# A decode block on one core: 112-column quadrants, a folded second mean, and differently cut MLP weight loads

## The chip, the core and the metric

The kernel runs on one core of a Trainium2 chip. The metric is the device time in microseconds (us) of one execution, the median over the timed runs. Engines are named as the profile names them: PE is TensorE's matmul side and PEld its weight loads, DVE is VectorE, ACT is ScalarE, POOL is GpSimd, SP is SyncE, which here only issues DMAs. "SPq" is SP's queue of issued work.

## The reference

Four sequences (B = 4) with one new token each go through an attention over the last 1024 cached positions and then through an MLP. Both have a layer norm ahead of them and a residual sum behind them; the MLP is normalised twice, once outside and once inside.

```python
B, Sq, D = 4, 1, 448; Hq, Hkv, Sk, Dh = 16, 8, 4096, 256; F = 1792
W = min(4096, max(256, Sk // 4))                      # 1024
q = layernorm(x) @ wq
k, v = k_cache[:, :, Sk - W:], v_cache[:, :, Sk - W:] # 8 kv heads, each for two q heads
o = softmax(q @ k.T * Dh ** -0.5) @ v
h = x + o @ wo
y = layernorm(layernorm(h))
out = h + gelu(y @ w1 + b1) @ w2 + b2
```

All tensors are float32. K and V of the window are 33.6 MB each; with the weights some 88 MB are read once.

## The kernel before, in words

**Loading.** All large inputs come over SP's queue, in the order in which they are used. Twelve packed pieces called "stream" (`LOADS`, issued in `part`, L97) hold wq, K, V and wo of the heads in the order of their use; behind them come the last V (`v7`, two transfers), the last two heads' wo (`wo67`), the first MLP weights `w1` in two transfers (L373) and the second ones `w2` in four (L376). They go into a ring of three slots of equal size; a transfer into a slot is issued when the slot's last reader is done, so three slots' worth of transfers are under way or waiting at any time. Nothing else orders the loads.

**Heads.** For each of the 8 kv heads PE multiplies q by K (`scores`, L224), transposes the probabilities (L249), multiplies them by V (`values`, L261), transposes the result (`heads`, L286) and multiplies by wo (`project_o`). The order of PE's instructions is the order in which the program writes them; the other engines' order is set by the scheduler. A group of small products on zeros (`keep_warm`, L341) keeps PE busy between pieces of real work near the end.

**The tail.** The block's vector h has 4 x 448 numbers. They lie on 128 partitions: four quadrants of 32 partitions, one for each quarter j of the columns, with one of every 8 partitions holding a real row. In the kernel before a quadrant holds 128 columns: the quarters are columns 0 to 127, 128 to 255, 256 to 383, and 384 to 447 twice (64 columns, doubled by the function `columns`). Row sums over all quadrants come from a product with `fold`, which counts the doubled quarter by one half.

After the last wo product (`hsum`), DVE adds x and takes row sums (`h`, L411), PE turns these into the mean (L402), DVE subtracts it (`d`, L416), PE makes the second mean from the sums of d (L402), DVE subtracts it too (`z`, L421), PE transposes z by a product with picked columns of the identity (`pz`, L426), and DVE copies it into `zT` (L427), the weights of the first MLP product. ACT squares d and z for the two variances, which become the scale s beside the first MLP product (L438), and s is applied to the product's result together with b1 (L451), ahead of the GELU on ACT (L452).

The first MLP product runs over four slices of the 448 rows of w1. They are 128, 128, 128 and 64 rows; the last 64 rows are stored in two halves of columns on partitions 0 to 63 and 64 to 127 (`packed`), so that w1 fills 128 partitions x 6272 columns. The result u is transposed (`put`, L457 and L459), copied into `gT` (L461, L463) and multiplied by the 14 chunks of w2 (`py`, L469), 128 rows of w2 each, four products of 32 partitions a chunk. DVE adds h + b2 (`res`, L473) and SP stores the result (L474).

Of the kernel before, what the change touches and what calls it, by code (L numbers as in the profile page):

```python
# [8 lines left out]
F32 = mybir.dt.float32  # L9
# [6 lines left out]
B, D = 4, 448  # L16
# [14 lines left out]
QU = KV // 4  # L31
X0 = 2 * ND * B
V7A = 6 * B * DH
# [29 lines left out]
SLOT = max(sum(map(width, parts)) for parts in LOADS)  # L63
W1C = 3 * F + F // 2
EPS = 1e-5
# [3 lines left out]
def block_kernel(ctx: ExitStack, tc, rows, first, streams, v7, wo67, w1, w2, out):  # L69
# [82 lines left out]
    for j in range(4):  # L152
        nc.vector.tensor_scalar_mul(fold[: 3 * Q, j, :], sel[: 3 * Q, :], 1.0 / D)
        nc.vector.tensor_scalar_mul(fold[3 * Q :, j, :], sel[3 * Q :, :], 0.5 / D)
    fold = fold.rearrange("p j q -> p (j q)")
# [9 lines left out]

    b2b = const.tile([P, P], F32, name="b2b")
    nc.gpsimd.memset(b2b, 0.0)
    nc.scalar.dma_start(b2b[::GAP, :], rows)
    rs = const.tile([P, P + FQ], F32, name="rs")

    def spread(t):
        return t[..., ::GAP]
    xb, b1b = rs[:, :P], rs[:, P:]

# [96 lines left out]
    def columns(t, j):  # L271
        if j < 3:
            return t[:, j * P : (j + 1) * P].rearrange("p (i c) -> p i c", i=2)
        return t[:, None, 3 * P :].to_broadcast([t.shape[0], 2, H])

# [17 lines left out]
    def project_o(g, wt):  # L293
        for i in range(4):
            if g < HKV - 2:
                nc.tensor.matmul(  # L296
                    acc[i * Q : (i + 1) * Q, :], oT[g % 2][:, i, :], wt[:, i, :],
                    start=(g == 0), stop=(g == HKV - 3),
                )
                continue  # L300
            for j in range(4):
                nc.tensor.matmul(
                    ph[j * Q : (j + 1) * Q], oT[g % 2][:, i, :], columns(wt[:, i, :], j),
                    start=False, stop=(g == HKV - 1 and i == 3),
                )
# [14 lines left out]

    b1T = t0[:, WC + ND * B :].rearrange("p (c j) -> p c j", c=4)
    nc.vector.tensor_copy(spread(zT), xT)
    b1s = work.tile([P, 2 * 512], F32, tag="p", name="b1s")[:, : 4 * P]
# [8 lines left out]
    px = ps_s.tile([P, 512], F32, tag="s", name="px")  # L332
    nc.tensor.transpose(px[:, :P], zT.rearrange("p j q -> p (j q)"), ident)
    nc.vector.tensor_copy(xb, px[:, :P])

    tail = []

    def keep_warm(n, to=None):
        to = tail[0][:, 0, :] if to is None else to
        for _ in range(n):  # L340
            nc.tensor.matmul(to[:Q, :512], idle[:, :Q], idle, start=True, stop=True)  # L341
# [5 lines left out]
    for g in range(HKV):  # L347
        if g + 1 < HKV:
            p, rec_next = scores(g + 1)
            if g + 2 < HKV:  # L350
                project_q(g + 2, wq_parts(part("q", g + 2)))
            transpose_p(g + 1, p)
            if g + 1 == HKV - 2:
                keep_warm(10, ps_m.tile([P, 512], F32, tag="m", name="wait"))
            if g + 1 == HKV - 1:
                keep_warm(2, ps_m.tile([P, 512], F32, tag="m", name="wait"))
                tail.append(ps_t.tile([P, 2, 512], F32, tag="t", name="tail"))
                accs = once.tile([P, D], F32, tag="u", name="accs")
                nc.scalar.copy(accs, acc)
                keep_warm(8)  # L360
                hsum = ps_s.tile([P, 512], F32, tag="s", name="hsum")[:, :P]
                ph = hsum.rearrange("p (i c) -> p i c", i=2)
                pu = ps_s.tile([P, 512], F32, tag="s", name="pu")[:, :FQ]
                for j in range(4):
                    nc.tensor.matmul(ph[j * Q : (j + 1) * Q], sel, columns(accs, j), start=True, stop=False)
        else:
            v7t = load_v7()
            tw = slot("w1")
            wo_last = [wo_rows(tw[:, i * WC : (i + 1) * WC]) for i in range(2)]
            nc.sync.dma_start(tw[:, : 2 * WC], wo67)  # L370
            tw1 = tw[:, 2 * WC : 2 * WC + W1C]
            for a, n in ((0, 2 * F), (2 * F, W1C - 2 * F)):
                nc.sync.dma_start(tw1[:, a : a + n], w1[:, a : a + n])  # L373
            tw2 = slot("w2")
            for c0, n in ((0, 8), (8, 3), (11, 2), (13, 1)):
                nc.sync.dma_start(tw2[:, c0 * D : (c0 + n) * D], w2[:, c0 * D : (c0 + n) * D])  # L376
        if g == HKV - 1:
            keep_warm(8)
        po = values(g, v7t if g == HKV - 1 else None)
        heads(g, po, rec)  # L380
        if g < HKV - 2:
            project_o(g, wo_rows(part("o", g)))
        if g == HKV - 1:
            keep_warm(5)
            for i in range(2):
                project_o(HKV - 2 + i, wo_last[i])
        if g + 1 < HKV:
            rec = rec_next

    w1t = [tw1[:, a * F : (a + 1) * F] for a in range(3)] + [tw1[:, 3 * F :]]  # L390
    w2t = [tw2[:, c * D : (c + 1) * D] for c in range(NFC)]


    def w1_part(a, j):
        if a < 3:
            return slice(0, P), w1t[a][:, FQ * j : FQ * (j + 1)]
        rows = slice(H * (j // 2), H * (j // 2) + H)
        return rows, w1t[a][rows, FQ * (j % 2) : FQ * (j % 2 + 1)]


    def row_mean(sums, at, name):
        nc.tensor.matmul(at, fold, sums, start=True, stop=True)  # L402
        return at

    def stat(name):
        return once.tile([P, 1], F32, tag=name, name=name)

    keep_warm(3)
    h = once.tile([P, P], F32, tag="h", name="h")
    hs, ds, dv, zv = (stat(n) for n in ("hs", "ds", "dv", "zv"))  # L410
# [3 lines left out]
    keep_warm(2)  # L414
    d = once.tile([P, P], F32, tag="dh", name="dh")
    nc.vector.tensor_scalar(d, h, m, None, op0=ALU.subtract, op1=ALU.add, accum_out=ds)  # L416
    pm2 = ps_m.tile([P, 2], F32, tag="m", name="pm2")
    m = row_mean(ds, pm2[:, 0:1], "m2")
    keep_warm(2)
    z = once.tile([P, P], F32, tag="z", name="z")  # L420
    nc.vector.tensor_scalar(z, d, m, None, op0=ALU.subtract)  # L421
    junk = once.tile([P, P], F32, tag="junk", name="junk")
# [3 lines left out]
    nc.tensor.matmul(pz, z, rows_of, start=True, stop=True)  # L426
    nc.vector.tensor_copy(spread(zT), pz)  # L427
    hb = once.tile([P, P], F32, tag="hb", name="hb")
# [6 lines left out]
    for a in range(ND):  # L435
        for j in range(4):
            rows, w = w1_part(a, j)
            nc.tensor.matmul(  # L438
                pu[j * Q : (j + 1) * Q, :], zT[rows, a, :], w, start=(a == 0), stop=(a == ND - 1),
            )  # L440
        if a == 0:
            rsqrt(r1, row_mean(dv, tail[0][:, 1, 0:1], "v1"), "r1")
        if a == 1:
            v2 = stat("v2")
            nc.vector.tensor_scalar(v2, row_mean(zv, tail[0][:, 1, 1:2], "v2"), r1, r1, op0=ALU.mult, op1=ALU.mult)
            rsqrt(s, v2, "r2")
            nc.vector.tensor_mul(s, s, r1)


    for cols in (slice(0, 2 * P), slice(2 * P, FQ)):  # L450
        nc.vector.scalar_tensor_tensor(u[:, cols], pu[:, cols], s, b1b[:, cols], op0=ALU.mult, op1=ALU.add)  # L451
        nc.scalar.activation(u[:, cols], u[:, cols], AF.Gelu_apprx_tanh)  # L452

    keep_warm(5)
    put = ps_m.tile([P, 4, 4, B], F32, tag="m", name="put")
    for c in range(3):
# [5 lines left out]
    for i, rows in enumerate((slice(0, H), slice(H, P))):  # L462
        nc.vector.tensor_copy(spread(gT[rows, 12:, :]), put[rows, 3].rearrange("p (j i) q -> p j i q", i=2)[:, :, i, :])  # L463
    py = ps_o.tile([P, 2, H], F32, tag="o", name="py")
    for c in range(NFC):
        for j in range(4):
            n = 2 if c == 0 or j < 3 else 1
            w = columns(w2t[c], j) if n == 2 else w2t[c][:, None, 3 * P :]
            nc.tensor.matmul(  # L469
                py[j * Q : (j + 1) * Q, :n, :], gT[:, c, :], w, start=(c == 0), stop=(c == NFC - 1),  # L470
            )
    res = once.tile([P, P], F32, tag="res", name="res")
    nc.vector.tensor_add(res, py.rearrange("p i c -> p (i c)"), hb)  # L473
    nc.sync.dma_start(out, res)  # L474
# [73 lines left out]
```

## Time and profile before

| what | value |
|---|---|
| median of 3 runs (lowest, highest) | 214.31 us (214.24, 214.54) |
| time of the profiled execution | 214.15 us |
| its span, first to last instruction | 212.4 us |
| PE busy / DVE / ACT / POOL, share of the span | 70% / 17% / 12% / 2% |
| share of the DMA engines' time taken by SP's queue | 97.0% |
| mean transfer rate over the span | 416 GB/s |
| mean granted TensorE clock | 0.871 |

A span begins with the core's first instruction and ends with its last; the execution's time has 1.75 us more around it. A row of the timeline gives the start, the length, the engine, the line, the operation, what is written and read, the shape and the count; in brackets stands how long the engine had been idle before it and what ended that. "DMA w<-w" as the releaser means the landing of a transfer into one of the weight tiles.

### The profile page before, as it was taken

What the parts mean: (1) busy time and instruction counts of PE and PEld (TensorE: products, weight loads), DVE (VectorE), ACT (ScalarE), POOL (GpSimd) and SP (SyncE); (2) the same over time, 40 slices, a digit from 0 to 9 for tenths busy, and PEclk for the clock granted to TensorE, in tenths of its full rate; (3) what the DMA queues carried; (4) which work ended last, traced back from release to release, by engine and by line L of the source; (5) the groups of instructions that cost most, each with busy time, mean ns of one, the idle gap of its engine ahead of it and who ended that gap; (6) DMA issues with size and microseconds to landing.
All of it is one profiled execution on the core that took longest, in us unless ns stands there. A gap on an engine that the chain in (4) does not pass through costs nothing.

```text
span 212.4 us, 2546 instructions
## 1 busy us (share of the span) xinstructions
PE 148.5 (70%) x1102; PEld 57.2 (27%) x1102; DVE 36.2 (17%) x149; ACT 24.6 (12%) x58; POOL 5.1 (2%) x17
## 2 busy tenths in 40 slices
PE   0478815832891883980794780686999999999994
PEld 0332301300211520230222220141343334335443
DVE  1520310400111110320113011031130031101220
ACT  2011300300002100030003000030030102000310
POOL 5100000000000000000000000000000000000110
PEclk9999985995578599797579699599699999999999
DMA  7999899999989999999999999999999999999991
GB/s 296 438 406 509 350 499 414 427 436 418 479 385 464 427 414 430 417 479 403 446 446 403 446 414 461 426 426 397 454 412 426 432 423 415 424 416 424 424 386 67
DMA packets 3354, 88.45 MB, mean 416 GB/s; under 512 B 384, under 2 KB 656, under 8 KB 1040
## 3 DMA queue, kind: packets, MB, share of 16 engines
q1 hardware_dynamic: 3312, 88.29, 97.0%
q8 instruction: 8, 0.13, 0.2%
q14 instruction: 2, 0.02, 0.0%
q10 hardware_dynamic: 32, 0.01, 0.0%
HBM read 88.24 MB, written 0.07 MB: 416 GB/s over the span
## 4 chain that ended last, share of the span: by engine, by line
DMA 81%; PE 15%; SPq 1%; DVE 1%; issue 0%
DMA stream<-stream 70%; DMA w<-w 11%; PE s L224 6%; PE po L261 4%; PE acc L296 2%; PE pot L286 1%; PE pq L199 1%; PE py L469 0%; DVE o L278 0%; SPq L97 0%; SPq L376 0%; DVE oT L291 0%; SPq L95 0%; DVE res L473 0%
## 5 line engine op out<-in xcount | busy, mean ns | idle before, releaser
L224 PE MATMUL s<-stream,qT 128*32 128x512 f32 x256 | 40.0, 772 | 18.1 <-DMA stream<-stream 18.1
L261 PE MATMUL po<-stream,pT 128*32 128x512 f32 x224 | 30.6, 685 | 16.3 <-DMA stream<-stream 16.3
L224 PEld LDWEIGHTS s<-stream,qT 128*32 128x32 f32 x256 | 10.2, 139 | 45.1 <-issue 31.1
L228 DVE TENSOR_REDUCE mx<-s 128x1 f32<-128x512 f32 x16 | 11.1, 692 | 62.9 <-PE s L224 62.9
L261 PEld LDWEIGHTS po<-stream,pT 128*32 128x32 f32 x224 | 7.1, 120 | 33.4 <-DMA stream<-stream 18.9
L199 PE MATMUL pq<-stream,yT 128*32 128x512 f32 (+1 forms) x80 | 10.7, 630 | 7.6 <-DMA stream<-stream 4.7
L201 ACT COPY qs<-pq 128x512 f32<-128x512 f32 x8 | 4.7, 585 | 76.7 <-PE pq L199 76.7
L278 DVE TENSOR_SCALAR o<-po,rec 128x256 f32<-128x256 f32 x8 | 3.9, 484 | 54.9 <-PE po L261 54.9
L235 ACT ACTIVATE p<-s,nm 128x512 f32<-128x512 f32 x16 | 10.9, 689 | 15.8 <-DVE nm L231 15.8
L279 ACT ACTIVATE o<-po,rec 128x256 f32<-128x256 f32 x8 | 3.8, 474 | 69.6 <-DVE o L278 69.6
L249 PE MATMUL ppt<-ident,p 128*128 128x128 f32 x64 | 11.1, 303 | 0.2
L341 PEld LDWEIGHTS <-idle 128*32 128x32 bf16 x85 | 7.5, 96 | 11.5 <-issue 4.7
L286 PE MATMUL pot<-ident,o 128*128 128x128 f32 x32 | 7.7, 337 | 3.8 <-DVE o L278 3.1
L207 PE MATMUL pqt<-ident,qs 128*128 128x128 f32 x32 | 6.1, 323 | 5.6 <-ACT qs L201 5.6
L341 PE MATMUL tail<-idle 128*32 128x512 bf16 x37 | 9.4, 381 | 0.0
L296 PE MATMUL acc<-stream,oT 128*32 128x448 f32 x48 | 7.5, 698 | 2.5 <-DVE oT L291 1.4
L249 PEld LDWEIGHTS ppt<-ident,p 128*128 128x128 f32 x64 | 7.6, 151 | 3.8 <-ACT p L235 3.8
L199 PEld LDWEIGHTS pq<-stream,yT 128*32 128x32 f32 x80 | 4.4, 128 | 15.4 <-issue 14.5
L286 PEld LDWEIGHTS pot<-ident,o 128*128 128x128 f32 x32 | 3.6, 157 | 13.3 <-DVE o L278 10.7
L207 PEld LDWEIGHTS pqt<-ident,qs 128*128 128x128 f32 x32 | 3.9, 159 | 10.2 <-ACT qs L201 8.5
L193 POOL TENSOR_TENSOR r<-ve_r,mhalf 128x1 f32<-128x1 f32 x2 | 1.1, 543 | 191.5 <-DVE ve_r L192 191.5
L210 DVE TENSOR_REDUCE q<-pqt 128x16 f32<-128x64 f32 x8 | 1.8, 224 | 16.8 <-PE pqt L207 16.8
(110 smaller groups left out, 79.1 us busy)
## 6 DMA issues: line engine op xcount, KB each, us to landing
stream<-stream SPq DMA_DIRECT2D x5, 7040.0 KB, 39.1
stream<-stream SPq DMA_DIRECT2D x2, 6912.0 KB, 40.5
stream<-stream SPq DMA_DIRECT2D x2, 4992.0 KB, 24.3
stream<-stream SPq DMA_DIRECT2D x2, 4096.0 KB, 24.1
stream<-stream SPq DMA_DIRECT2D x1, 5888.0 KB, 36.4
w<-w SPq DMA_DIRECT2D x2, 1792.0 KB, 23.1
v<-v SPq DMA_DIRECT2D x1, 3072.0 KB, 20.1
w<-wo SPq DMA_DIRECT2D x1, 1792.0 KB, 20.1
```

What stands on the lines that cost most here:

```text
L199: nc.tensor.matmul(pq[j * Q : (j + 1) * Q, cols], yT[:, a, :], w, start=True, stop=True)
L201: nc.scalar.copy(qs, pq)
L207: nc.tensor.transpose(pt[:, i * P : (i + 1) * P], qs[:, i * P : (i + 1) * P], ident)
L224: nc.tensor.matmul(s[h][b * Q : (b + 1) * Q, :], qT[g % 2][:, c, b, :], load_k(g, h, c)[:, b, :], start=(c == 0), stop=(c == 1),)
L228: nc.vector.reduce_max(mx[:, h : h + 1], s[h], axis=AX.X)
L235: nc.scalar.activation(p[:, h * 512 : (h + 1) * 512], s[h], AF.Exp, bias=nm, scale=SCALE, accum_out=sums[:, h : h + 1],)
L249: nc.tensor.transpose(pt[:, c, :], p[:, c * P : (c + 1) * P], ident)
L261: nc.tensor.matmul(po[b * Q : (b + 1) * Q], pT[g % 2][:, c, b, :], vt[:, :, b, :], start=(c == 0), stop=(c == NKC // 2 - 1),)
L278: nc.vector.tensor_scalar_mul(o[:, :, :P], po[:, :, :P], rec)
L286: nc.tensor.transpose(pt[:, at : at + P], o[:, i, c * P : (c + 1) * P], ident)
L296: nc.tensor.matmul(acc[i * Q : (i + 1) * Q, :], oT[g % 2][:, i, :], wt[:, i, :], start=(g == 0), stop=(g == HKV - 3),)
L341: nc.tensor.matmul(to[:Q, :512], idle[:, :Q], idle, start=True, stop=True)
```

## The change

Four things are changed together.

1. **Quadrants of 112 columns.** 448 = 4 x 112, so each quadrant now holds a true quarter and no column is doubled. `fold` is the same in all rows. The products into `hsum` and `py` are 112 columns wide for each quadrant, and DVE's and ACT's operations of the tail work on 112 columns. x is carried a second time in the first load, cut in quarters of 112 (16 more columns of 128 rows). The result keeps its 128 columns in the store; the 16 behind are zeros that POOL writes ahead of time.
2. **The second mean is subtracted inside the transposing product.** PE transposes d rather than z, and a second product that accumulates into the same `pz` subtracts the second mean (weights from the sums of d, and `foldn`, which is the negative of `fold`). z itself is still made for its variance, behind.
3. **w1 on 112 partitions.** Four slices of 112 rows, 112 partitions x 7168 columns, in two transfers of 4608 and 2560 columns. The third slice's first 256 columns of each quarter come with the first transfer.
4. **w2 in pieces of 8, 4, 1.5 and 0.5 chunks** in place of 8, 3, 2 and 1. The last chunk's product is made in two halves of 56 columns.

```diff
-X0 = 2 * ND * B
+X0 = 3 * ND * B
+C = D // 4
-W1C = 3 * F + F // 2
+W1C = 4 * F
+W1A = 2 * F + 4 * 2 * P
...
+    foldn = const.tile([P, 4, B], F32, name="foldn")
+    nc.vector.tensor_scalar_mul(foldn, fold.rearrange("p j (b e) -> p j b e", b=B)[..., 0], -1.0)
...
-            for a, n in ((0, 2 * F), (2 * F, W1C - 2 * F)):
-                nc.sync.dma_start(tw1[:, a : a + n], w1[:, a : a + n])
+            for a, e in ((0, W1A), (W1A, W1C)):
+                nc.sync.dma_start(tw1[:C, a:e], w1[:, a:e])
...
-            for c0, n in ((0, 8), (8, 3), (11, 2), (13, 1)):
-                nc.sync.dma_start(tw2[:, c0 * D : (c0 + n) * D], w2[:, c0 * D : (c0 + n) * D])
+            for a, e in ((0, 16), (16, 24), (24, 27), (27, 28)):
+                nc.sync.dma_start(tw2[:, a * 2 * C : e * 2 * C], w2[:, a * 2 * C : e * 2 * C])
...
+    pz = ps_m.tile([P, 4, B], F32, tag="m", name="pz")
+    nc.tensor.matmul(pz[:C], d, rows_of, start=True, stop=False)
+    nc.tensor.matmul(pz[:C], ds.to_broadcast([P, C]), foldn, start=False, stop=True)
+    nc.vector.tensor_copy(spread(zT[:C]), pz[:C])
     pm2 = ps_m.tile([P, 2], F32, tag="m", name="pm2")
     m = row_mean(ds, pm2[:, 0:1], "m2")
-    keep_warm(2)
...
-    pz = ps_m.tile([P, 4, B], F32, tag="m", name="pz")
-    nc.tensor.matmul(pz, z, rows_of, start=True, stop=True)
-    nc.vector.tensor_copy(spread(zT), pz)
...
-    keep_warm(2)
+    keep_warm(4)
...
+    for a, half in ((2, 0), (2, 1), (3, None)):
+        first_layer(a, half)
...
+    for half in range(2):
+        for j in range(4):
+            nc.tensor.matmul(
+                py[j * Q : (j + 1) * Q, half * C // 2 : (half + 1) * C // 2], gT[:, NFC - 1, :],
+                w2_last[half][:, j * C // 2 : (j + 1) * C // 2], start=False, stop=(half == 1),
+            )
+    nc.vector.tensor_add(res[:, :C], py, hb)
```

SP issues the same transfers in the same order; the last of them differ in shape. From `wo67` on they stood like this before (a "w" tile is w1's or w2's slot, the shape is partitions x elements of 4 bytes):

```order
L370 DMA w_937<-wo 128x3584
L373 DMA w_937<-w 128x3584
L373 DMA w_937<-w 128x2688
L376 DMA w_941<-w 128x3584
L376 DMA w_941<-w 128x1344
L376 DMA w_941<-w 128x896
L376 DMA w_941<-w 128x448
L474 DMA out<-res 128x128
```

and now:

```order
L371 DMA w_935<-wo 128x3584
L374 DMA w_935<-w 112x4608
L374 DMA w_935<-w 112x2560
L377 DMA w_939<-w 128x3584
L377 DMA w_939<-w 128x1792
L377 DMA w_939<-w 128x672
L377 DMA w_939<-w 128x224
L489 DMA out<-res 128x128
```

The two transfers of w1 hold as many bytes as before on 16 partitions fewer, with rows of 18432 and 10240 bytes in place of 14336 and 10752; the last transfer of w2 is half as long.

On PE, from the second mean to the first MLP product (`ds` are the sums of d, `pz` the transposed vector, `tail<-idle` the small products on zeros), there stood before:

```order
L402 MATMUL pm_1036<-ds,fold 128x1
L341 LDWEIGHTS idle
L341 MATMUL tail<-idle 32x512
L341 LDWEIGHTS idle
L341 MATMUL tail<-idle 32x512
L426 MATMUL pz<-ident,z 128x16
L341 LDWEIGHTS idle
L341 MATMUL tail<-idle 32x512
L341 LDWEIGHTS idle
L341 MATMUL tail<-idle 32x512
L438 MATMUL pu<-w_937,zT 32x448 x4
```

and now:

```order
L424 MATMUL pz<-ident,dh 112x16
L425 MATMUL pz<-foldn,ds 112x16
L408 MATMUL pm_1038<-ds,fold 128x1
L343 LDWEIGHTS idle
L343 MATMUL tail<-idle 32x512
L343 LDWEIGHTS idle
L343 MATMUL tail<-idle 32x512
L343 LDWEIGHTS idle
L343 MATMUL tail<-idle 32x512
L343 LDWEIGHTS idle
L343 MATMUL tail<-idle 32x512
L445 MATMUL pu<-w_935,zT 32x448 x4
```

The transposing product has moved ahead of the second mean and has become two; all four small products now stand between the second mean and the first MLP product.

At PE's end, from the transposition of u on, now stand these rows, with the last chunk's eight half products apart:

```order
L343 MATMUL tail<-idle 32x512
L469 MATMUL put<-ident,u 128x16 x3
L471 MATMUL put<-ident,u 64x16 x2
L479 MATMUL py<-w_939,gT 32x112 x52
L484 MATMUL py<-w_939,gT 32x56 x8
```

Before, `py` had 56 products: three of 128 columns and one of 64 for each chunk but the first, which had four of 128. It now has 60.

More of the change, by code (lines that the diff above doesn't have):

```diff
@@ L302, in project_o @@
                 nc.tensor.matmul(
-                    ph[j * Q : (j + 1) * Q], oT[g % 2][:, i, :], columns(wt[:, i, :], j),
+                    hsum[j * Q : (j + 1) * Q], oT[g % 2][:, i, :], columns(wt[:, i, :], j),
                     start=False, stop=(g == HKV - 1 and i == 3),
@@ L332, in block_kernel @@
     px = ps_s.tile([P, 512], F32, tag="s", name="px")
-    nc.tensor.transpose(px[:, :P], zT.rearrange("p j q -> p (j q)"), ident)
-    nc.vector.tensor_copy(xb, px[:, :P])
+    nc.tensor.transpose(px[:, :C], zT[:C].rearrange("p j q -> p (j q)"), ident[:C, :C])
+    nc.vector.tensor_copy(xb, px[:, :C])
     tail = []
@@ L360, in block_kernel @@
                 keep_warm(8)
-                hsum = ps_s.tile([P, 512], F32, tag="s", name="hsum")[:, :P]
-                ph = hsum.rearrange("p (i c) -> p i c", i=2)
+                hsum = ps_s.tile([P, 512], F32, tag="s", name="hsum")[:, :C]
                 pu = ps_s.tile([P, 512], F32, tag="s", name="pu")[:, :FQ]
                 for j in range(4):
-                    nc.tensor.matmul(ph[j * Q : (j + 1) * Q], sel, columns(accs, j), start=True, stop=False)
+                    nc.tensor.matmul(hsum[j * Q : (j + 1) * Q], sel, columns(accs, j), start=True, stop=False)
         else:
@@ L388, in block_kernel, with w1_part @@
             rec = rec_next
[L390 to L398, printed above, removed]
+    w1_cols = [(slice(0, 2 * P), W1A - 4 * 2 * P), (slice(2 * P, FQ), W1A)]
+    def w1_part(a, j, half):
+        if a < 2:
+            at = a * F + j * FQ
+        elif a == 3:
+            at = W1C - F + j * FQ
+        else:
+            cols, at = w1_cols[half]
+            n = cols.stop - cols.start
+            return tw1[:C, at + j * n : at + (j + 1) * n]
+        return tw1[:C, at : at + FQ] if half is None else tw1[:C, at : at + FQ][:, w1_cols[half][0]]
+    w2t = [tw2[:, c * D : (c + 1) * D] for c in range(NFC - 1)]
+    w2_last = [tw2[:, ((NFC - 1) * 2 + i) * 2 * C :][:, : 2 * C] for i in range(2)]
     def row_mean(sums, at, name):
@@ L434, in block_kernel, with first_layer @@
     u = once.tile([P, FQ], F32, tag="u", name="u")
-    for a in range(ND):
+    def first_layer(a, half=None):
+        cols = slice(0, FQ) if half is None else w1_cols[half][0]
         for j in range(4):
-            rows, w = w1_part(a, j)
             nc.tensor.matmul(
-                pu[j * Q : (j + 1) * Q, :], zT[rows, a, :], w, start=(a == 0), stop=(a == ND - 1),
+                pu[j * Q : (j + 1) * Q, cols], zT[:C, a, :], w1_part(a, j, half), start=(a == 0), stop=(a == ND - 1),
             )
[L441 to L450, printed above, removed]
+    first_layer(0)
+    rsqrt(r1, row_mean(dv, tail[0][:, 1, 0:1], "v1"), "r1")
+    first_layer(1)
+    v2 = stat("v2")
+    nc.vector.tensor_scalar(v2, row_mean(zv, tail[0][:, 1, 1:2], "v2"), r1, r1, op0=ALU.mult, op1=ALU.mult)
+    rsqrt(s, v2, "r2")
+    nc.vector.tensor_mul(s, s, r1)
+    for a, half in ((2, 0), (2, 1), (3, None)):
+        first_layer(a, half)
+    for cols, _ in w1_cols:
         nc.vector.scalar_tensor_tensor(u[:, cols], pu[:, cols], s, b1b[:, cols], op0=ALU.mult, op1=ALU.add)
@@ L454, in block_kernel @@
     keep_warm(5)
+    res = once.tile([P, P], F32, tag="res", name="res")
+    nc.gpsimd.memset(res, 0.0)
     put = ps_m.tile([P, 4, 4, B], F32, tag="m", name="put")
@@ L463, in block_kernel @@
         nc.vector.tensor_copy(spread(gT[rows, 12:, :]), put[rows, 3].rearrange("p (j i) q -> p j i q", i=2)[:, :, i, :])
-    py = ps_o.tile([P, 2, H], F32, tag="o", name="py")
-    for c in range(NFC):
+    py = ps_o.tile([P, C], F32, tag="o", name="py")
+    for c in range(NFC - 1):
         for j in range(4):
-            n = 2 if c == 0 or j < 3 else 1
-            w = columns(w2t[c], j) if n == 2 else w2t[c][:, None, 3 * P :]
             nc.tensor.matmul(
-                py[j * Q : (j + 1) * Q, :n, :], gT[:, c, :], w, start=(c == 0), stop=(c == NFC - 1),
+                py[j * Q : (j + 1) * Q], gT[:, c, :], columns(w2t[c], j), start=(c == 0), stop=False,
             )
-    res = once.tile([P, P], F32, tag="res", name="res")
-    nc.vector.tensor_add(res, py.rearrange("p i c -> p (i c)"), hb)
+    for half in range(2):
[5 more added lines that the diff above has]
+    nc.vector.tensor_add(res[:, :C], py, hb)
     nc.sync.dma_start(out, res)
@@ L505 @@
     b1[:, :FQ] = np.asarray(B_b1).reshape(4, FQ)
-    first = np.concatenate([wq[0], xT, b1.reshape(4, 4, P).transpose(2, 1, 0).reshape(P, 16)], axis=1)
+    xr = np.zeros((P, 4 * B), np.float32)
+    xr[:C] = x.reshape(B, 4, C).transpose(2, 1, 0).reshape(C, 4 * B)
+    first = np.concatenate([wq[0], xT, xr, b1.reshape(4, 4, P).transpose(2, 1, 0).reshape(P, 16)], axis=1)
     def part(kind, g, i):
@@ L545 @@
     r = run(nc, [arrays], core_ids=[0])
[L546 to L547 removed]
+    got = np.asarray(r.results[0]["out"]).reshape(4, B, GAP, P)[:, :, 0, :C]
+    return np.ascontiguousarray(got.transpose(1, 0, 2).reshape(B, 1, D))
```

39 lines of the change are left out of this document (19 added, 20 removed).

## The prediction

> **What bounds the kernel now.** I read the page's parts 1 to 4 first, then the chain of waits at its end, and then the timeline of the last 15 us.
>
> ```profile
> span 212.4 us, 2546 instructions
> PE 148.5 (70%) x1102; PEld 57.2 (27%) x1102; DVE 36.2 (17%) x149; ACT 24.6 (12%) x58; POOL 5.1 (2%) x17
> ...
> DMA  7999899999989999999999999999999999999991
> ...
> q1 hardware_dynamic: 3312, 88.29, 97.0%
> ...
> DMA 81%; PE 15%; SPq 1%; DVE 1%; issue 0%
> ```
>
> The DMA engines are busy in every slice from the first to the last but one; 97.0% of their time goes to SP's queue, and 81% of the chain that ended last is transfers. No compute engine comes near that. So what decides is the bytes, the rate at which they move, and what happens after the last of them has landed. A table by stage gives the rate:
>
> ```profile
> core 0: us, PE busy (x) PEld busy (x) DVE busy (x) ACT busy (x) POOL busy (x), PEclk, DMA share, GB/s
> 4.00:206.00 202.00, 144.99 (x994) 54.44 (x998) 35.03 (x142) 24.58 (x58) 2.11 (x3) 0.86 1.00 431
> 206.00:208.70 2.70, 2.64 (x92) 2.37 (x96) 0.06 (x1) 0.00 (x0) 0.00 (x0) 1.00 0.62 234
> ```
>
> From 4 to 206 us the engines are full (share 1.00, 431 GB/s); in the last 2.7 us only 0.62 of their time is used. They do not finish together. The chain's end and the timeline's end show what the landing releases:
>
> ```profile
> 184.43 24.13 DMA w<-w
> 208.56 0.04 issue
> 208.60 1.05 PE py L469 x12
> 209.65 0.02 issue
> 209.67 0.29 DVE res L473
> ```
>
> ```profile
> 205.91 2.36 PEld L469 LDWEIGHTS py<-w,gT 128*32 128x32 f32 x88 [0.46 <-issue]
> 205.94 3.66 PE L469 MATMUL py<-w,gT 128*32 128x128 f32 x112 [0.39 <-DVE gT L461]
> 208.60 0.37 PEld L469 LDWEIGHTS py<-w,gT 128*32 128x32 f32 x16 [0.33 <-DMA w<-w]
> 209.18 0.16 PEld L469 LDWEIGHTS py<-w,gT 128*32 128x32 f32 x8 [0.21 <-DMA w<-w]
> 209.67 0.29 DVE L473 TENSOR_TENSOR res<-py,hb 128x128 f32<-128x128 f32 x1 [3.61 <-PE py L469]
> 209.99 0.35 SPq L474 DMA_DIRECT2D out<-res  x1
> ```
>
> PE has done 11 chunks of w2 by 208.27 and waits 0.33 us for the piece with two chunks, does these, and waits 0.21 us for the last one, which lands just ahead of 209.18. From there 0.49 us to the sum `res`, 0.32 us to the store. PE's lead over the transfers is therefore only some 0.3 us: the transfers bound the kernel, with PE close behind.
>
> **The change part by part.**
>
> *Bytes.* The first load is 16 columns of 128 rows longer: 8192 B at 431 GB/s, +0.02 us. w1 has 128 x 6272 elements before and 112 x 7168 now, both 802,816 elements or 3.211 MB; w2 has the same bytes. At 431 GB/s w1 takes 7.45 us. If rate and bytes stay, this step is worth 0.
>
> *The rate of a transfer of 112 rows* is what the trace cannot show, since every large transfer in it has 128 rows: the 3312 packets of SP's queue are 23 transfers of 144, one packet for each of 128 rows and one for each of 16 engines. So 8 rows go to an engine, if evenly. 112 rows are 7 an engine, an even split, with rows of 28,672 B instead of 25,088 B in all. From below: 0, the engine has the same bytes. A gain by the split alone is excluded, as the share is 1.00 already. From above: if the 431 GB/s are not what 16 engines carry but what 128 partitions take in (3.37 GB/s each), 112 partitions take in 7/8, and w1 lasts 8/7 as long: 7.45 / 7, +1.06 us. If two engines must then share a group of partitions all the time, w1 takes twice as long, +7.45 us; half the time, +3.7 us. The nearest rows are the full windows at 1.00, which belong to the engines as much as to the partitions. I take 0, since the row counts engines' busy time and that is what is full; it is the weakest step here.
>
> [...]
>
> *The second mean.* These rows of the timeline carry it:
>
> ```profile
> 196.88 0.35 DVE L416 TENSOR_SCALAR_CACHE_REDUCE dh<-h,pm 128x128 f32<-128x128 f32 x1 [0.29 <-PE pm L402]
> 197.30 0.30 PEld L402 LDWEIGHTS pm<-ds,fold 128*128 128x128 f32 x2 [0.42 <-DVE dh L416]
> 197.61 0.60 PE L341 MATMUL tail<-idle 128*32 128x512 bf16 x2
> 197.72 0.29 DVE L421 TENSOR_SCALAR z<-dh,pm 128x128 f32<-128x128 f32 x1 [0.49 <-PE pm L402]
> 198.15 0.30 PEld L426 LDWEIGHTS pz<-ident,z 128*128 128x128 f32 x2 [0.42 <-DVE z L421]
> 198.47 0.60 PE L341 MATMUL tail<-idle 128*32 128x512 bf16 x2
> 198.82 0.21 PEld L438 LDWEIGHTS pu<-w,zT 128*32 128x32 f32 x8 [0.24 <-DVE zT L427]
> 201.52 1.84 PE L438 MATMUL pu<-w,zT 128*32 128x448 f32 x16 [0.18 <-DMA w<-w]
> ```
>
> One full-width product takes PE 0.31 us (197.30 to 197.61). Now three stand in a row from 197.3: `pz` twice, then the mean, to 198.2; behind them four small products at 0.18 to 0.22 us each (198.47 to 198.82 for two; nine take 2.12 us in the row below), so the first MLP product starts at 198.9 to 199.1 instead of 198.82. zT itself is ready at about 198.3, earlier by 0.5 us, but PE is not free, and w1 is hardly there:
>
> ```profile
> 185.06 2.12 PE L341 MATMUL tail<-idle 128*32 128x512 bf16 x9
> L373 SPq DMA_DIRECT2D w<-w x2: 426/930/1435, 174.2 to 175.7; - x2
> DMA to landing us min/median/max: 24.0/24.9/25.8
> ```
>
> w1's first part was issued at 174.2 and landed 24.0 us later, at 198.2, the second at 175.7 + 25.8 = 201.5, where PE's row of 201.52 waits for it. The first part now has 0.229 MB more, 0.53 us, so 198.7. The second lands at 201.5 as before. The product runs 2.45 us for two slices with the two variances between (198.82 to 201.27, 0.25 us ahead of the landing), then 1.77 us to 203.29. From 199.0 that would be 201.45 and, with the third slice's first half already there and no wait, 203.2 to 203.4 with 0.1 us for the split slice: no gain, no loss. The 0.5 us that the folded mean wins goes into the small products. What is late next if this slips is the GELU, then gT, then `py`, which had 0.33 us of cover.
>
> *w2's pieces and the end.* 11 chunks take 2.36 us of weight loads, 0.215 us a chunk, 0.027 us a load; columns do not enter while loads set the pace. `py` starts at 205.9 to 206.1 as before. The piece of 8 lands earlier; the piece of 4 holds chunk 11, so PE runs 12 chunks through to 208.5 to 208.7. The last two landings were 0.58 us apart for 224 KB; for 112 KB that is 0.29, so the piece of 1.5 chunks lands at 209.14 - 0.29 = 208.85 and PE waits for it. Then 1.5 chunks are 16 loads, 0.43 us at most (0.32 if half-wide products went faster): PE is through at 209.2 to 209.3, when the last half chunk has already landed at 209.14. Its 8 loads and the drain take 0.49 us at most and 0.4 us at least. So `py` ends at 209.6 to 209.8 instead of 209.67: from -0.1 to +0.13. I take 0. `res` on 112 columns: DVE's 128x256 and 128x192 forms of L451 differ by 75 ns, 1.2 ns a column,
>
> ```profile
> L451 DVE SCALAR_TENSOR_TENSOR u<-pu,r,rs 128x256 f32<-128x256 f32 x1 | 0.5, 484 | 0.7 <-PE pu L438 0.7
> L451 DVE SCALAR_TENSOR_TENSOR u<-pu,r,rs 128x192 f32<-128x192 f32 x1 | 0.4, 409 | 0.0
> ```
>
> so 16 columns are -0.02 us. The narrower products into `hsum` lie before w1's landing and win nothing; the zeros of `res` are written by POOL, 2% busy; the store is as large as before.
>
> **Sum:** +0.02 + 0 + 0 + 0 - 0.02 = 0. On the profiled execution 214.15 us (span 212.4 and 1.75 around it); it stood 0.16 us under the median, so 214.3 us.
>
> **The rivals.**
>
> *Transfers onto 112 partitions are slower* (ends slower). Place: w1's two transfers, behind them all of w2 in the same queue. For it: in the trace rate, engines and partitions always go together, so the limit may be the partitions'. Against it: the even split over engines, the share of 1.00 that counts engines. Two prices: +1.06 us, 215.4 us, if the rate goes with partitions; +3.7 us, 218.0 us, if engines also get in each other's way half the time (up to 221.8 in the worst case). It decides from 6% loss of rate on w1 on, which is 0.43 us or 0.2%. [...]
>
> *The last transfers end sooner* (faster). Only 0.62 of the engines' time is used in the last 2.7 us, 1.0 us is lost there; new row lengths and pieces could let the late engines end with the others. Half of it is 0.5 us: 213.8 us. Against it: each engine still gets an equal share of each transfer.
>
> *PE becomes the bound.* If the four small products and three full ones start the first MLP product 0.3 us late and `py` inherits that, its lead is gone: +0.3 us at most, 214.6 us, still hardly outside 0.2%. It decides when the row of `py` no longer shows a wait for a transfer.
>
> **How the numbers follow.** A measurement of this kernel can tell about 0.2% (0.43 us) from no change. No change 0.46 (214.3 us, own range 214.0 to 214.6); w1 slower by the partitions 0.22; w1 slower by more 0.12; PE late and just over the bound 0.04; faster 0.16. So faster 0.16, same 0.46, slower 0.38. The range takes in the faster case's 213.8 and reaches up to just under 218, leaving out about 1 in 10 above and less below: 213.7 to 217.8.
>
> **What would show each step.** w1's rate: its two landings 198.7 and 201.5, seen in the wait of the first MLP product's later slices, and a rate near 431 GB/s from 198 to 206 us. If w1 is slower, these slices wait for a transfer past 202 us, the windows there show less than 400 GB/s, and everything behind is late by the same amount. Mean: `pz` at 197.3, first MLP product at 198.9 to 199.1. Pieces: one wait for a transfer in `py` at 208.85, none or a tiny one for the last half chunk, `py` over at 209.6 to 209.8. The prediction is wrong if the DMA share falls between 190 and 206 us, or if the last landing moves by more than 0.3 us either way.

## The result, and the profile after

The changed kernel takes 223.75 us (223.04 to 224.27, 6 runs) against 214.30 us before: a ratio of 1.0436, 95% interval 1.0420 to 1.0453, some 9.4 us slower. The prediction of 214.3 us (213.7 to 217.8) is wrong. The profiled execution took 223.04 us with a span of 221.2 us, 8.8 us more than the span before. Two executions lie far from the other ten of their kernel, 273.46 us with the pieces of w2 alone and 224.41 us with the second mean alone, and the ratios below leave them out.

The page of the changed kernel, parts 1 to 4 (the row "GB/s" has one figure for each of the 40 slices of 5.5 us):

```profile
span 221.2 us, 2582 instructions
...
DMA  7998998999999999999998999999999999999991
GB/s 286 463 448 387 489 428 387 482 418 400 470 411 407 471 416 410 460 465 397 428 468 387 448 445 417 417 438 400 444 427 433 424 424 405 373 247 190 246 386 54
...
q1 hardware_dynamic: 3280, 88.30, 97.0%
...
DMA 76%; PE 20%; ACT 1%; SPq 1%; issue 1%; DVE 0%; ACTq 0%
```

Up to slice 34, 188 us, nothing differs. Then the rate falls to 373, 247, 190 and 246 GB/s, while the digits of the DMA row stay at 9: the engines are busy and move half as much. The table by stage says the same; first the kernel before, from 194 to 206 us:

```profile
194.00:206.00 12.00, 11.43 (x134) 5.83 (x138) 3.38 (x16) 2.77 (x7) 1.09 (x2) 1.00 0.99 415
```

and the changed one in five stretches (PE clock, DMA share and GB/s are the last three figures):

```profile
4.00:186.00 182.00, 126.08 (x810) 45.48 (x811) 30.08 (x121) 21.33 (x50) 1.18 (x2) 0.85 1.00 432
186.00:191.00 5.00, 4.88 (x40) 1.68 (x38) 0.00 (x0) 0.00 (x0) 0.00 (x0) 1.00 1.03 431
194.00:206.00 12.00, 7.05 (x88) 4.63 (x89) 1.37 (x7) 2.06 (x5) 0.00 (x0) 0.86 0.99 211
206.00:214.00 8.00, 7.90 (x49) 2.66 (x41) 1.56 (x6) 0.69 (x2) 1.09 (x2) 0.57 0.98 333
217.00:217.50 0.50, 0.50 (x32) 0.50 (x26) 0.00 (x0) 0.00 (x0) 0.00 (x0) 1.00 0.06 20
```

211 GB/s at a share of 0.99, against 415 GB/s at the same share. The last traffic falls between 217.0 and 217.5 us. In the kernel before it had ended by 208.8:

```profile
208.00:208.80 0.80, 0.74 (x27) 0.47 (x24) 0.00 (x0) 0.00 (x0) 0.00 (x0) 1.00 0.29 105
208.80:209.70 0.90, 0.80 (x24) 0.33 (x16) 0.03 (x1) 0.00 (x0) 0.00 (x0) 1.00 0.00 0
```

So the transfers run out some 8.5 us later. The timeline of the tail shows what waits:

```profile
196.03 2.61 PEld L303 LDWEIGHTS hsum<-w,oT 128*32 128x32 f32 x64 [2.45 <-DMA w<-wo]
205.56 0.19 PEld L445 LDWEIGHTS pu<-w,zT 112*32 112x32 f32 x8 [3.47 <-issue]
205.59 0.96 PE L445 MATMUL pu<-w,zT 112*32 112x448 f32 x8 [3.00 <-DMA w<-w]
206.97 1.72 PE L445 MATMUL pu<-w,zT 112*32 112x448 f32 x8
210.31 0.84 PEld L445 LDWEIGHTS pu<-w,zT 112*32 112x32 f32 x16 [0.97 <-DMA w<-w]
215.54 2.70 PE L479 MATMUL py<-w,gT 128*32 128x112 f32 x104 [0.39 <-issue]
218.49 0.28 DVE L488 TENSOR_TENSOR res<-py,hb 128x112 f32<-128x112 f32 x1 [2.83 <-PE py L484]
```

w1's first transfer lands at 205.5 us (198.2 before), its second at 210.3 (201.5 before): 8.8 us late, the whole of the longer span. Even `wo67`, a transfer on 128 partitions ahead of w1 in the queue, comes 2.1 us late: `hsum` starts at 196.03, and in the kernel before, whose timeline had

```profile
193.94 1.69 PEld L302 LDWEIGHTS hsum<-w,oT 128*32 128x32 f32 x64 [0.54 <-DMA w<-wo]
```

at 193.94. The chain that ended last goes through w1's second landing, and behind it through PE alone:

```profile
174.75 35.52 DMA w<-w
210.27 0.04 issue
210.31 2.36 PE pu L445 x16
```

From the second landing to `res` PE needs 8.18 us, almost the same as before (8.15 us, 201.52 to 209.67), but differently: the products of `py` wait for no transfer now, and PE is slow. It had waited 3.00 us for w1 (3.47 us without a weight load), its granted clock from 206 to 214 us is 0.57, and a block of eight passes of the first MLP product takes 1.72 us instead of the 0.96 of the block ahead.

The clock was low behind a shorter wait as well: ahead of `hsum` PE waited 1.95 us, until 196.03 us, and the clock, 1.00 from 186 to 194 us, was 0.79 on the mean in these two stretches:

```profile
194.00:198.00 4.00, 2.05 (x49) 1.97 (x52) 0.00 (x0) 0.00 (x0) 0.00 (x0) 0.79 1.00 234
198.00:202.00 4.00, 4.00 (x40) 2.38 (x33) 1.37 (x7) 0.39 (x2) 0.00 (x0) 0.79 1.02 218
```

### The profile page after: what moved, and what is told of

The parts are those of the page before. It is cut to its first block, busy times and chain, and to the rows that moved or that the text cites. A ratio compares the mean times of both kernels' runs of the same rounds, so it can differ in the third digit from the quotient of the medians.

```text
span 221.2 us, 2582 instructions
## 1 busy us (share of the span) xinstructions
PE 152.8 (69%) x1120; PEld 59.2 (27%) x1120; DVE 35.3 (16%) x146; ACT 24.6 (11%) x58; POOL 5.2 (2%) x18
## 3 DMA queue, kind: packets, MB, share of 16 engines
q1 hardware_dynamic: 3280, 88.30, 97.0%
## 4 chain that ended last, share of the span: by engine, by line
DMA 76%; PE 20%; ACT 1%; SPq 1%; issue 1%; DVE 0%; ACTq 0%
DMA stream<-stream 60%; DMA w<-w 16%; PE s L227 9%; PE po L264 4%; PE ppt L252 2%; PE pq L202 1%; PE py L479 1%; PE pu L445 1%; PE pqt L210 1%; ACT qs L204 1%; PE tail L343 1%; PE put L469 0%; SPq L374 0%; SPq L99 0%; SPq L97 0%
## 5 line engine op out<-in xcount | busy, mean ns | idle before, releaser
L264 PE MATMUL po<-stream,pT 128*32 128x512 f32 x224 | 30.0, 676 | 14.3 <-DMA stream<-stream 14.3
L343 PEld LDWEIGHTS <-idle 128*32 128x32 bf16 x85 | 8.0, 101 | 12.6 <-issue 6.0
L343 PE MATMUL tail<-idle 128*32 128x512 bf16 x37 | 10.1, 409 | 0.0
L297 PE MATMUL acc<-stream,oT 128*32 128x448 f32 x48 | 8.0, 752 | 3.0 <-DMA stream<-stream 1.5
L445 PE MATMUL pu<-w,zT 112*32 112x448 f32 (+2 forms) x40 | 6.1, 723 | 3.1 <-DMA w<-w 3.0
```

The costliest lines, as they stand in the source:

```text
L264: nc.tensor.matmul(po[b * Q : (b + 1) * Q], pT[g % 2][:, c, b, :], vt[:, :, b, :], start=(c == 0), stop=(c == NKC // 2 - 1),)
L297: nc.tensor.matmul(acc[i * Q : (i + 1) * Q, :], oT[g % 2][:, i, :], wt[:, i, :], start=(g == 0), stop=(g == HKV - 3),)
L445: nc.tensor.matmul(pu[j * Q : (j + 1) * Q, cols], zT[:C, a, :], w1_part(a, j, half), start=(a == 0), stop=(a == ND - 1),)
```

## The experiments

Two theories stood at first: "partitions" (transfers that do not fill the 128 partitions are slow) and "source" (the new array's rows lie badly in HBM), with a third, "PE", that PE's new order holds up the tail. A run below that has no ratio was executed once.

**Zeros under w1.** The changed kernel with w1 filled up to 128 rows:

```diff
-                nc.sync.dma_start(tw1[:C, a:e], w1[:, a:e])
+                nc.sync.dma_start(tw1[:, a:e], w1[:, a:e])
...
+    w1 = np.concatenate([w1, np.zeros((P - C, W1C), np.float32)], axis=0)
```

> The changed kernel, with 16 rows of zeros under w1, so that its two transfers fill 128 partitions (128 x 4608 and 128 x 2560): 0.459 MB more, the rest of the change as it is. Theory 'partitions' (a transfer onto 112 partitions makes engines meet on the same partitions, and runs at half the rate): the rate is back at 431 GB/s, the extra bytes cost 1.06 us, so 214.3 + 1.1 = 215.4 us. Theory 'source' (the new array has rows 28,672 B apart in HBM, and these are read slowly): no change by this, 223.8 us or 1 to 2 us more. Theory 'PE' (the four small products and the new order of the tail hold it up, the transfers only follow): about 223 us.

215.53 us, ratio 1.0055 (1.0039 to 1.0072). In its stretch of 194 to 206 us stands

```profile
194.00:206.00 12.00, 11.24 (x138) 5.90 (x137) 2.93 (x13) 2.75 (x7) 1.09 (x2) 1.00 0.99 417
```

Sixteen more partitions and 0.459 MB more make the kernel 8.2 us faster than without them. The rows still lie 28,672 B apart, and PE's program is the same, so "source" and "PE" fall here. The packet records of the two traces show where the time went: a row of w1's first transfer, 18,432 B, keeps its engine for 1.28 us on the mean in the changed kernel and for 0.69 us here. `hsum`, which waits for `wo67`, starts at 194.29 us here, against 196.03 in the changed kernel.

**The kernel before, w1 cut by partitions.** Nothing of the change but the cut:

```diff
-                nc.sync.dma_start(tw1[:, a : a + n], w1[:, a : a + n])
+                for r0, r1 in ((0, 112), (112, P)):
+                    nc.sync.dma_start(tw1[r0:r1, a : a + n], w1[r0:r1, a : a + n])
```

> The kernel before, with each of w1's two transfers cut into partitions 0-111 and 112-127; same array, same bytes, nothing else of the change. Theory 'partitions': 7/8 of w1 at half rate costs 6.5 to 8 us, 16 rows more on top, 221 to 226 us. Theory 'source': 214.3 to 215 us. Theory 'PE': 214.3 to 215 us.

225.77 us, 11.4 us over the kernel before, within the 221 to 226 us expected under "partitions". From 194 to 206 us it moves 221 GB/s at a share of 1.04:

```profile
194.00:206.00 12.00, 6.43 (x88) 3.41 (x87) 1.43 (x7) 2.09 (x5) 0.00 (x0) 0.84 1.04 221
```

The cut alone, without any other part of the change, makes a loss of this size; the two transfers of 16 partitions have a share in the 11.4 us.

**Another distance of the rows in HBM.**

```diff
+    w1 = np.concatenate([w1, np.zeros((C, 896), np.float32)], axis=1)
```

> The changed kernel with w1's rows 32,256 B apart in HBM instead of 28,672 (896 unused columns that are not loaded), still 112 partitions and the same bytes. Theory 'partitions': 223 to 224.5 us as it is. Theory 'source': 214 to 216 us.

223.14 us, as the changed kernel. "Source" falls a second time.

**Which cuts are slow.** Six stream loads of the kernel before, cut into blocks of neighbouring partitions:

```diff
+ROWS = {
+    1: ((0, 112), (112, 128)), 3: ((0, 96), (96, 128)), 5: ((0, 64), (64, 128)),
+    7: ((0, 120), (120, 128)), 9: ((0, 80), (80, 128)), 11: ((16, 128), (0, 16)),
+}
...
-            nc.sync.dma_start(t[:, at : at + src.shape[-1]], src)
+            for r0, r1 in ROWS.get(len(LOADS) - len(streams) - 1, ((0, P),)):
+                nc.sync.dma_start(t[r0:r1, at : at + src.shape[-1]], src[r0:r1])
```

> The kernel before, with six of its twelve stream loads cut by partitions into two transfers each: 112+16, 96+32, 64+64, 120+8, 80+48, and partitions 16-127 ahead of 0-15; same bytes, same source arrays, same columns. Between two of them stands an uncut load. Theory 'partitions': while a cut load runs the rate falls to 200 to 300 GB/s, for 112 rows to about 220 as in the changed kernel, for 64+64 to half; each costs 7 to 16 us, the whole some 250 to 300 us. Theory 'source' or 'the new array': the rate stays near 430 GB/s, the whole at 214 to 217 us.

341.31 us, above the 250 to 300 us expected. In the table by stage the stretches follow the loads in their order: 112 and then 16 partitions in one row; 96 (and the start of 32); an uncut load; 64 with 64; 120; 8, with the beginning of the next uncut load; 80; the 112 partitions from 16 on.

```profile
17.00:48.00 31.00, 9.01 (x54) 3.27 (x54) 2.79 (x11) 1.94 (x5) 0.00 (x0) 0.71 0.98 207
75.00:95.00 20.00, 7.70 (x48) 2.05 (x44) 2.69 (x8) 1.92 (x5) 0.00 (x0) 0.67 0.97 207
105.00:113.00 8.00, 7.29 (x42) 3.58 (x41) 0.77 (x5) 0.59 (x1) 0.00 (x0) 0.58 0.97 417
120.00:150.00 30.00, 10.65 (x70) 3.46 (x70) 2.79 (x11) 1.94 (x5) 0.00 (x0) 0.70 0.99 205
175.00:200.00 25.00, 9.58 (x60) 2.40 (x60) 1.37 (x3) 0.47 (x1) 0.00 (x0) 0.74 0.99 207
206.00:214.00 8.00, 0.00 (x0) 0.00 (x0) 0.00 (x0) 0.00 (x0) 0.00 (x0) 0.50 0.86 106
235.00:245.00 10.00, 7.26 (x52) 2.41 (x53) 1.63 (x4) 0.08 (x1) 0.00 (x0) 0.68 0.98 201
275.00:288.00 13.00, 8.73 (x48) 2.76 (x52) 0.81 (x2) 0.58 (x2) 0.00 (x0) 0.78 1.01 223
```

Every block of 64 to 120 neighbouring partitions runs at 201 to 223 GB/s, about half of an uncut load, with all engines busy (0.97 to 1.01). The 106 GB/s are not the rate of the 8 partitions alone: that stretch moves 0.85 MB, and their eight rows of 56,320 B are 0.45 MB of it at most.

**Other patterns of partitions.** The same loads, cut by a step instead of a block:

```diff
+ROWS = {
+    1: [slice(16 * i, 16 * i + 16) for i in range(8)],
+    3: [slice(i, P, 8) for i in range(8)],
+    5: [slice(32 * i, 32 * i + 32) for i in range(4)],
+    7: [slice(i, P, 4) for i in range(4)],
+    9: [slice(i, 7 * 16, 7) for i in range(7)] + [slice(7 * 16, P)],
+    11: [slice(i, P, 2) for i in range(2)],
+}
```

> The kernel before, with six of its twelve stream loads cut by partitions in other ways, an uncut load between any two: 8 transfers of 16 neighbouring partitions; 8 of every eighth partition; 4 of 32 neighbours; 4 of every fourth; 7 of every seventh partition (of 112) and one of the last 16; 2 of every second. [...] Theory 'all or nothing' (any transfer that does not fill 128 partitions runs at half the rate, however it lies): about 210 GB/s for all six.

322.6 us. By stage: 16 neighbours; an uncut load; every eighth; 32 neighbours; a stretch with every fourth between two uncut loads; every seventh of 112; every second, with uncut loads on both sides.

```profile
22.00:72.00 50.00, 5.68 (x46) 2.38 (x38) 2.79 (x11) 1.94 (x5) 0.00 (x0) 0.61 1.06 119
82.00:92.00 10.00, 8.02 (x51) 2.89 (x51) 2.25 (x8) 1.94 (x5) 0.00 (x0) 0.72 1.01 435
100.00:130.00 30.00, 10.25 (x60) 2.50 (x60) 2.70 (x8) 1.92 (x5) 0.00 (x0) 0.61 1.00 206
152.00:178.00 26.00, 10.62 (x70) 3.46 (x70) 2.79 (x11) 1.94 (x5) 0.00 (x0) 0.77 0.99 203
195.00:230.00 35.00, 23.02 (x147) 7.42 (x151) 4.99 (x17) 2.88 (x7) 0.00 (x0) 0.79 0.99 428
240.00:250.00 10.00, 6.06 (x40) 1.83 (x44) 0.69 (x1) 0.00 (x0) 0.00 (x0) 0.66 1.03 240
268.00:285.00 17.00, 15.54 (x102) 5.67 (x103) 2.37 (x6) 1.37 (x3) 0.00 (x0) 0.89 0.99 423
```

A quarter of the rate (119 GB/s), a half (203 to 240), the full rate (423 to 435): the pattern decides, not the number of partitions. 32 neighbours are slow (203), 32 partitions four apart are as fast as an uncut load (428). "All or nothing" falls. The shares of 0.99 to 1.06 say that the engines are all busy in the slow stretches too; each row takes longer: by the packet records a row of 56,320 B takes 2.08 us in an uncut load and 7.94 us in the loads of 16 neighbours. What holds a row up there no trace shows. That the rate goes with which partitions a transfer takes together is what the next two expectations call "groups".

**112 partitions in scattered parts.** If patterns decide, every fourth partition should help the changed kernel:

```diff
-                nc.sync.dma_start(tw1[:C, a:e], w1[:, a:e])
+                for i in range(4):
+                    nc.sync.dma_start(tw1[i:C:4, a:e], w1[i::4, a:e])
```

> The changed kernel with each of w1's two transfers cut into four, of every fourth of the 112 partitions (28 each): same 112 partitions, same bytes, no zeros added. In the stream loads of the run before, transfers of every fourth partition ran at 433 GB/s. Theory 'groups': it is which partitions are reached together, not that there are 112 of them; 28 rows go to 14 engines at most, so 7/8 of the rate, w1 lasts 7.45 x 8/7, and the time is 214.3 + 1.06 = 215.4 us. Rival (112 partitions at half the rate however they are cut): 223 to 224 us.

223.4 us, ratio 1.0436 (1.0404 to 1.0469): no gain, against the 215.4 us expected under "groups". (The stretch shown above has 428 GB/s where this expectation says 433.) With two parts of every second partition:

> The same with two transfers each, of every second of the 112 partitions (56 each). Theory 'groups': 56 rows go to 14 engines too, 215.4 us, or up to 2 us more if engines meet at times. Rival: 223 to 224 us.

224.92 us, no gain either, with 221 to 227 GB/s from 194 to 206 us. In the run with fourths the rate from 194 to 206 us is better than in the changed kernel, but far from 7/8:

```profile
194.00:206.00 12.00, 7.27 (x96) 3.97 (x99) 1.37 (x7) 2.06 (x5) 0.00 (x0) 0.90 0.94 262
...
206.00:210.00 4.00, 4.00 (x30) 1.53 (x34) 0.75 (x4) 0.00 (x0) 1.08 (x2) 0.50 1.00 326
```

and the chain's end shows why not even that is seen in the time:

```profile
203.62 0.14 issue
203.75 1.72 PE pu L446 x8
205.47 0.52 PE tail L409 x2
205.99 1.65 PE pu L446 x8
```

w1's first part landed at 203.6, 2 us earlier than in the changed kernel, and from there on the chain is PE's alone, at a clock of 0.50 from 206 to 210 us. What the transfers won, PE gave back. The packets tell how the rows were dealt: SP's queue has 3360 of them here, 21 transfers of 144 and 8 of 42, that is 28 rows and 14 engines each, read as in the prediction as one packet a row and one an engine; in the changed kernel 3280, 21 of 144 and 2 of 128, that is 112 rows and 16 engines.

**The same with 32 rows a transfer.** To tell the dealing from the number of transfers: zeros under w1 again, and both transfers in fourths.

```diff
-                nc.sync.dma_start(tw1[:, a:e], w1[:, a:e])
+                for i in range(4):
+                    nc.sync.dma_start(tw1[i::4, a:e], w1[i::4, a:e])
```

> The changed kernel with 16 rows of zeros under w1 (128 partitions) and each of its two transfers cut into four of every fourth partition, 32 rows each: against the run of every fourth of 112 partitions (223.4 us) only four rows more in each transfer, 32 instead of 28, so that it goes to 16 engines with two rows each instead of 14. Theory 'dealing' (the rate hangs on how the rows of a transfer fall to engines, and is full where every engine stays on partitions of its own, as in the stream loads of every fourth of 128 partitions): 215.5 us, as with zeros and uncut. Rival (eight transfers of scattered partitions are slow at this place, by their number or their issue): 222 to 225 us.

215.94 us, ratio 1.0092 (1.0061 to 1.0123), 0.4 us over what "dealing" expected, and

```profile
194.00:206.00 12.00, 11.22 (x140) 5.98 (x140) 2.93 (x13) 2.75 (x7) 1.09 (x2) 1.00 0.99 414
```

Four rows more in each of eight transfers, and w1 runs at the full rate. SP issues the eight transfers over the same time in both runs, the last at 195.6 us with 28 rows and at 194.2 with 32. Neither the number of transfers nor the scattered partitions are slow; 28 rows on 14 engines are (262 GB/s), 32 on 16 are not (414). That every engine stayed on partitions of its own, as "dealing" has it, no trace shows.

**The other parts of the change.** Pieces of 8, 4, 1.5 and 0.5 chunks, alone, in the kernel before:

```diff
-            for c0, n in ((0, 8), (8, 3), (11, 2), (13, 1)):
-                nc.sync.dma_start(tw2[:, c0 * D : (c0 + n) * D], w2[:, c0 * D : (c0 + n) * D])
+            for a, e in ((0, 16), (16, 24), (24, 27), (27, 28)):
+                nc.sync.dma_start(tw2[:, a * C2 : e * C2], w2[:, a * C2 : e * C2])
```

> The kernel before with the fourth part of the change alone: w2 in pieces of 8, 4, 1.5 and 0.5 chunks, the last chunk in two halves. By the prediction's step on the pieces: the end of the last product moves by -0.1 to +0.13 us, 214.2 to 214.5 us. A rival (the last, shorter piece lets the kernel end sooner by the 0.29 us that half a chunk takes to arrive): 214.0 us.

214.35 us, ratio 1.0001 (0.9993 to 1.0010): nothing, as the step said; the rival of 214.0 us falls.

The second mean inside the transposing product, alone:

```diff
+    nc.tensor.matmul(pz, d, rows_of, start=True, stop=False)
+    nc.tensor.matmul(pz, ds.to_broadcast([P, P]), foldn, start=False, stop=True)
+    nc.vector.tensor_copy(spread(zT), pz)
...
-    keep_warm(2)
+    keep_warm(4)
```

> The kernel before with the second part alone: the second mean subtracted by a second product into pz, four small products behind it. By the prediction's step: the first MLP product starts at 198.9 to 199.1 instead of 198.82, waits for w1's second landing as before, no change: 214.2 to 214.4 us. A rival (PE's lead of 0.3 us is lost): up to 214.6 us.

214.16 us, ratio 0.9993 (0.9985 to 1.0002): no difference that can be told. Its timeline has the step nearly as it was worked out:

```profile
197.45 0.30 PEld L420 LDWEIGHTS pz<-ident,dh 128*128 128x128 f32 x2 [0.42 <-DVE dh L418]
198.11 0.19 DVE L422 COPY zT<-pz 128x16 f32<-128x16 f32 x1 [0.72 <-PE pz L421]
198.66 0.54 PEld L440 LDWEIGHTS pu<-w,zT 128*32 128x32 f32 x8
201.62 0.16 PEld L440 LDWEIGHTS pu<-w,zT 128*32 128x32 f32 x8 [0.19 <-DMA w<-w]
```

Both together:

> Both of these, without the quadrants of 112 columns and with w1 on 128 partitions. If the steps are right: the sum of the two, 214.0 to 214.5 us. It is also the version without the slow transfer that might beat both kernels.

214.82 us, ratio 1.0016 (1.0007 to 1.0024). Its eleven runs fall into two groups, four at 214.07 to 214.36 us and seven at 214.74 to 214.94 us; their spans are the same, 212.3 to 212.6 and 212.3 to 212.5 us, so the second group's extra time lies outside the span from the first instruction to the last, and what makes it is open. The version does not beat the kernel before, and lies 0.3 us over the upper end of what was expected. Its timeline has one wait of `py` for a transfer, ahead of the piece of four chunks, and none behind it:

```profile
208.01 1.12 PEld L472 LDWEIGHTS py<-w,gT 128*32 128x32 f32 x40 [0.38 <-DMA w<-w]
```

And the price of bytes, in the kernel before with 896 columns more in w1's second transfer:

```diff
-            for a, n in ((0, 2 * F), (2 * F, W1C - 2 * F)):
+            for a, n in ((0, 2 * F), (2 * F, W1C + H * 14 - 2 * F)):
```

> The kernel before with w1's second transfer 896 columns longer (zeros that nothing reads), 128 x 7168 elements for w1 as in the changed kernel with zeros under w1: 0.459 MB more at full rate. If bytes and rate are all: 214.3 + 1.06 = 215.4 us, and the difference to the 215.53 us of that kernel, 0.1 us, is what the other three parts of the change are worth.

215.36 us, ratio 1.0062 (1.0043 to 1.0080): 1.08 us for 0.459 MB. The changed kernel with zeros under w1 moves the same bytes in 215.53 us; that is 0.17 us more, inside the two intervals, so the quadrants, the mean and the pieces together make no difference that can be told. The quadrants were not run alone. No version tried beats the kernel before by more than can be told; the nearest is the mean alone, 0.1 us under it.

## Why the prediction was wrong, point by point

- **What bounds the kernel**: right for the kernel before. In the changed one the chain still goes through transfers, but only up to w1's second landing, which is 8.8 us late; behind it PE alone takes as long as PE and the last transfers did before.
- **Bytes at 431 GB/s**: right where the rate stays: at that rate 0.459 MB take 1.06 us, and 1.08 us were measured.
- **"The rate of a transfer of 112 rows": this step failed.** I took 0, with the reason that the row "counts engines' busy time and that is what is full". The changed kernel has the share of the kernel before, 0.99, at 211 GB/s instead of 415: each row kept its engine nearly twice as long (1.28 us, against 0.69 with zeros under w1), and that counts as busy. So the full share was no evidence that engines are the limit. The even split, 7 rows an engine, says nothing either; 3280 packets fit 112 rows on 16 engines, as I assumed, and the rate was half all the same. For the same reason one sign of being wrong, a falling DMA share between 190 and 206 us, stayed silent; less than 400 GB/s there and slices that wait past 202 us, the signs of the rival, both came.
- **The upper bound** was too low as well. Two engines on one group all the time was priced at w1's own time again, +7.45 us. No run shows two engines on one group; measured were 8.8 us at w1's second landing. Neighbours were held up as well: `wo67`, ahead of w1 and on all 128 partitions, came 2.1 us late; how much of the difference this makes is not separated. The range had stopped at half of that price.
- **The rival "transfers onto 112 partitions are slower"** had the right place at a chance of 0.34, and the runs bear it out (223.75 us with 112 partitions, 215.53 with 16 rows of zeros under them); both its prices, 1.06 and 3.7 us, were too small, and its worst case of 221.8 us as well. That engines get in each other's way, on which the second price and the worst case rest, was my estimate; no trace shows it.
- **The second mean**: right in its worth. zT was said for 198.3 and came at 198.3 (198.11 + 0.19); the first MLP product was said for 198.9 to 199.1 and began at 198.66, 0.2 to 0.4 us sooner; it waited for the second landing, here until 201.62. No gain, no loss.
- **The pieces of w2**: right in the sum, -0.1 to +0.13 us said, 0.0 measured. The wait was in another place: said for 208.85 ahead of the piece of 1.5 chunks, it ended at 208.01 ahead of the piece of four in the run of both parts.
- **PE as the bound**: a rival at 0.3 us that was priced without the clock. Where transfers came late, PE waited, its clock was low behind the wait, and then it was the bound: in the changed kernel (3.00 us of waiting, a clock of 0.57 from 206 to 214 us) from w1's second landing on, where `py` no longer waits for a transfer, and in the run of fourths (0.50 from 206 to 210 us) for all that the transfers had won.
- **The last transfers end sooner**: did not happen.

Open: which rows go to which engine in a transfer that is not 128 partitions, and so why 28 rows of every fourth partition run at 262 GB/s where 32 run at 414; the profile does not say which engine moved a packet. Open too is whether the partitions written or the rows read together set the rate, since every run takes the same rows on both sides; that another distance of the rows in HBM changed nothing, and that rows from 10,240 to 56,320 B were all slow in the slow patterns (10,240 B kept an engine for 0.80 us in the changed kernel, where 16 engines at 431 GB/s would take 0.38; 56,320 B for 7.94 us with 16 neighbours, against 2.08 uncut), speaks for the partitions.

## What to carry to other kernels

Where loads fill the DMA engines' time (here a share of 1.00 at 431 GB/s), try to fill all 128 partitions, with zeros if need be: the changed kernel with 16 partitions of zeros stood 1.2 us over the kernel before, and 9.4 without them. (Every second or every fourth of 128 partitions did as well as all of them here: 423 and 428 GB/s in the cut stream loads, 435 in an uncut one.) A full DMA share told here that engines were busy, not what they moved: 0.99 stood beside 211 GB/s and beside 415. Read it together with the GB/s. Before a layout is changed from 128 partitions, one load of the new shape put into the old kernel tells the price roughly: here 11.4 us for the cut alone, with its 16 partitions apart, and 9.4 for the change.

## What the runs showed of the hardware that was not expected

- Loads in blocks of 64, 80, 96, 112 or 120 neighbouring partitions ran at 201 to 223 GB/s, like 32 (203); 16 neighbours ran at 119; every second or fourth partition of 128 at 423 to 428, as an uncut load (435).
- A full transfer that was under way beside the slow ones in the same queue came late too (`wo67` by 2.1 us; by 0.35 with zeros under w1).
- 28 rows to a transfer went, by the packet counts, to 14 engines, and this was slow (262 GB/s); 32 rows to 16 engines were not (414).
- The late transfer cost a second time: after some 3 us of waiting TensorE's clock was 0.57, and a block of products behind took 1.72 us instead of 0.96.
